# Scales that are powers of two: one chain on VectorE in place of a chain on two engines

## The chip, the cores and the metric

One core of a Trainium2 chip runs the kernel. The metric is device time in microseconds of one execution; runs are compared by their median. The core has a matrix engine (TensorE, "PE" in the profile; its weight loads are "PEld"), VectorE ("DVE"), ScalarE ("ACT"), GpSimd ("POOL") and SyncE ("SP"). Each engine works off its own instructions in the order of the program, and waits on semaphores for the others. In this kernel SP and POOL only issue transfers.

## The reference: a gated long convolution beside a feed-forward layer

For 2048 positions of 1024 channels, with `xn` the layer norm of `A_q`:

```python
k_shift = sum(k_pad[:, t:t + S, :] * shift_k[:, ks - 1 - t] for t in range(ks))   # four taps
kv = k_shift * v
y = irfft(rfft(kv_pad) * rfft(ssm_k_pad))[:S] + kv * ssm_D     # causal convolution over 2048 positions
A = xn * y
B = silu(xn @ w1) @ w2                                         # 1024 -> 3584 -> 1024
return A_q + A + B
```

All is in float32. The kernel gets there with half-precision matmuls: each operand is multiplied by a scale and split into a float16 high part and a float16 remainder, and three products of these parts are summed. The scales are powers of two, so they change nothing but the exponent, and they are found from the data: squares are summed, the sum's exponent is halved by shifting its bits, and the result and its reciprocal become the factors by which parts are scaled and outputs scaled back.

## The kernel before: streams, an order made by a planner, and the scales

**Order.** The program is written as some thirty Python generators ("streams"), each of which yields operations (class `Op`) and conditions (tokens and flags). A planner (class `Order`, lines 118 to 206) keeps a clock for each engine. Again and again it takes the operation that could start first by its estimate, less a bias of its stream (0.0 to 0.26 us), emits it, and moves the engine's clock by the operation's estimated time. That gives one fixed order of instructions for each engine. An estimate that changes can so move instructions that have nothing to do with it. An `Op` may emit several instructions, which then stand together.

**Stages.** First the layer norm, transposes and splits of x. Beside it the 14 column pairs of `w1` are loaded, squared and summed, scaled and split (`scales_w1`, line 713, and `factors_w1`, line 762); pairs 0 and 1 are used as they are, the other twelve in a seven-product form of a 2 x 2 block product. TensorE runs `xn @ w1` in two halves (lines 941 to 1017), then the product with `w2` (lines 1045 to 1064), and at the end eight units of the seven-product form (`units2`, line 1092). ScalarE and VectorE evacuate its results, split them again, and make the parts of `w2`.

**The convolution** runs beside this from some 200 us on, in eight groups of 128 channels (line 1350 and after). For each group: `gate` (line 1407) applies the taps and multiplies by v, with squares summed on ScalarE; `signal_parts` splits; `stage1` makes the first part of a transform on TensorE, and `to_spec` copies it out; `forward`, `product` and `inverse` are long VectorE instructions on the tile `spec`; `energy` sums squares of the product on ScalarE; `result_scales` (line 1617) makes the scales of the result; `result_parts` splits; `stage1_inv` transforms back on TensorE; `gated` (line 1719) applies scales row tile by row tile, multiplies by the normed x, and writes out. From the fifth group on that write is a transfer that adds to the output in DRAM, issued by POOL.

**The end.** The last unit of the feed-forward part (`evacuate2`, lines 1139 to 1184) reads one output tile back (line 1175), after all convolution outputs are there (flag "conv out"), adds it to its own result, and writes without adding. Its other results go out as adding transfers from POOL, in the same queue as those of the convolution.

**The scales.** Two routines make them. `norm` (line 446): a matmul with ones sums over the partitions into PSUM; then one `Op` on VectorE reduces, takes the maximum with 1e-30, shifts, and runs the caller's `then`, all in one piece. `norm_on_two` (line 482): the same matmul; ScalarE sums up the columns (each sum an activation and a read of the accumulator, with the tile `tiny` as a bias that keeps the sum above zero); VectorE shifts and takes a reciprocal (lines 495 and 497); ScalarE multiplies by constants (`small`, line 478, one activation each, L480 in the profile). `norm` serves w1's pairs 0 and 1 and the norm of w2; `norm_on_two` serves the pairs after that (twelve), the gate (eight) and the result (eight). The factors go into `wsc` for w1 and into `csc` (`sc` in the code) for a group; columns 8 to 23 of `sc` hold the result's factor times each row tile's reciprocal deviation (`rstd`), which `gated` takes as scales.

Of the kernel before, what the change touches and what calls it, by code (L numbers as in the profile page):

```python
# [11 lines left out]
F32 = mybir.dt.float32  # L12
BF16 = mybir.dt.bfloat16
F16 = mybir.dt.float16
I32 = mybir.dt.int32
AF = mybir.ActivationFunctionType
ALU = mybir.AluOpType
AX = mybir.AxisListType
ADD, SUB, MUL = ALU.add, ALU.subtract, ALU.mult

P = 128
# [9 lines left out]
W = 512  # L31
# [269 lines left out]
def h3_ffn_kernel(ctx, tc, x, kp, vs, fs, shift, dskip, w1, w2, cfwd, cinv, out):  # L301
# [23 lines left out]
    def V(f, o, ins, us=None, m=0.15):  # L325
        return Op("DVE", us or 1.03 * (size(o) / 960 + 0.075), 0.16, f, ins, [o], m)
# [4 lines left out]
    def T(f, o, ins, us, m=0.1):  # L331
        return Op("PE", us, 0.3, f, ins, [o], m)
# [22 lines left out]
    def a_act(o, i, func, scale=1.0, bias=None, total=None):  # L355
        def f():
            kw = {} if bias is None else {"bias": bias}
            if total is not None:
                kw["accum_out"] = total
            nc.scalar.activation(o, i, func, scale=scale, **kw)  # L360
        ins = [i] + [s for s in (scale, bias) if s is not None and not isinstance(s, float)]
        p = A(f, o, ins)
        p.table = func if func in (AF.Silu, AF.Sqrt) else None
        p.busy += 0.07 * (len(ins) - 1) - 0.06 * (i.space == bass.MemoryType.PSUM)
        if total is not None:
            p.busy += 0.19
            p.writes.append(total)
        return p
# [29 lines left out]
    for n, e in enumerate((14 - 64, 10 - 64, 8 - 64, 64 - 23, 64)):  # L398
        nc.vector.memset(powers[:, n:n + 1], 2.0 ** e)
    invc = cst.tile([P, 1], F32, name="invc")  # L400
    tiny = cst.tile([P, 1], F32, name="tiny")
    nc.vector.memset(tiny, 2.0 ** -100)
    eps = cst.tile([P, 1], F32, name="eps")
    nc.vector.memset(eps, EPS)
    one = cst.tile([P, 1], F32, name="one")
# [40 lines left out]
    def norm(ring, ss, ns, then, flags, margin=1.5):  # L446

        yield ring.ready
        pt, tok = ring.tile([P, W])
        yield pw.ready  # L450
        e, etok = pw.tile([P, 16])

        cols, n = len(ns), sum(ns)

        def mm():
            nc.tensor.matmul(pt[:, 0:n], ones, ss, start=True, stop=True)

        def chain():
            for c, m in enumerate(ns):
                q = sum(ns[:c])  # L460
                if m > 1:
                    nc.vector.tensor_reduce(e[:, c:c + 1], pt[:, q:q + m], axis=AX.X, op=ADD)
                else:
                    nc.vector.tensor_copy(e[:, c:c + 1], pt[:, q:q + 1])
            pow2(e[:, 0:cols], e[:, 0:cols])
            then(e[:, 0:cols])

        yield T(mm, pt[:, 0:n], [ss], 0.25, m=margin)
        p = V(chain, e, [pt[:, 0:n]], us=1.1)
        p.writes = p.writes + flags[0]  # L470
        yield p
        tok.set()
        etok.set()
        for t in flags[1]:
            t.set()


    def small(o, i, scale, ins=()):

        return Op("ACT", 0.2, 0.2, lambda: nc.scalar.activation(o, i, AF.Copy, scale=scale), [i, *ins], [o], 0.15)  # L480

    def norm_on_two(ring, ss, ns, then, flags, margin=1.5):

        yield ring.ready
        pt, tok = ring.tile([P, W])
        yield pw.ready
        e, etok = pw.tile([P, 16])
        cols, n = len(ns), sum(ns)

        def mm():  # L490
            nc.tensor.matmul(pt[:, 0:n], ones, ss, start=True, stop=True)

        def halved():
            a, r = e[:, 0:cols], e[:, 2:2 + cols]
            nc.vector.tensor_scalar(a.bitcast(I32), a.bitcast(I32), 24, 23,
                                    op0=ALU.logical_shift_right, op1=ALU.logical_shift_left)
            nc.vector.reciprocal(r, a)

        yield T(mm, pt[:, 0:n], [ss], 0.25, m=margin)
        for c, m in enumerate(ns):  # L500
            q = sum(ns[:c])
            p = a_act(e[:, 8:8 + m], pt[:, q:q + m], AF.Identity, 1.0, tiny, total=e[:, c:c + 1])
            p.busy = 0.4
            yield p
        tok.set()
        yield V(halved, e[:, 0:4], [e[:, 0:2]], us=0.34)
        yield from then(e[:, 0:cols], e[:, 2:2 + cols])
        etok.set()
        for t in flags:
            t.set()  # L510


# [200 lines left out]
    def scales_w1():  # L713
        for n, (_, i) in enumerate(pairs):
            yield (0.25, 0.16, 0.1, 0.05)[min(n, 3)]
            m = 4 if n < 2 else 2
            if n >= NP:
                for a in range(m):
                    yield flag["raw", n, a]
                flag["scaled", n].set()  # L720
                continue
            yield sq_r.ready
            ss, tok = sq_r.tile([P, 4])
            for a in range(m):
                yield flag["raw", n, a]
                r = raws[n][2][a]
                yield a_act(junk[:, 0:r.shape[1]], r, AF.Square, total=ss[:, a:a + 1])

            def then(e, i=i):
                sc = wsc[:, i]  # L730
                nc.vector.tensor_scalar(sc[:, 3:5], powers[:, 3:5], e, None, op0=MUL)
                nc.vector.reciprocal(e, e)
                nc.vector.tensor_scalar(sc[:, 0:3], powers[:, 0:3], e, None, op0=MUL)
            if n < 2:
                yield from norm(ctxs["nm"], ss[:, 0:m], (m,), then, ([wsc[:, i]], [flag["scaled", n], tok]))
                continue

            def scales(e, r, i=i):
                sc = wsc[:, i]
                yield small(sc[:, 3:5], powers[:, 3:5], e, [e])  # L740
                yield small(sc[:, 0:3], powers[:, 0:3], r, [r])
            yield from norm_on_two(ctxs["nm"], ss[:, 0:m], (m,), scales, [flag["scaled", n], tok])

    spills = []

# [604 lines left out]
    def convolution(floor):  # L1350
# [56 lines left out]
        def gate():  # L1407

            for g in range(NG):
                yield csc_r.ready  # L1410
                scs[g] = sc, _ = csc_r.tile([P, 8 + NT])
                yield css_r.ready
                sss[g] = ss, _ = css_r.tile([P, 12])
                yield flag["kf", g]
                kf, _ = kfs[g]
                yield acc_r.ready
                accs[g] = acc, _ = acc_r.tile([P, 2, T2, P])
                for a in range(2):
                    yield hi_r.ready
                    j, tok = hi_r.tile([P, T2, P], BF16)  # L1420
                    yield a_act(j, kf[:, a], AF.Square, total=ss[:, 4 + a:5 + a])
                    tok.set()

                flag["acc", g].set()
                tap = [taps[:, g, j:j + 1] for j in range(TAPS)]
                for b in range(2):
                    yield flag["kin", g, b]
                    kin, tok = kins.pop((g, b))
                    o = acc[:, b]
                    yield a_act(o, kin[:, 0:T2], AF.Copy, tap[HALO])  # L1430
                    for j in (2, 1, 0):
                        yield v_stt(o, kin[:, HALO - j:HALO - j + T2], tap[j], o, MUL, ADD)
                    tok.set()
                    for q in range(2):
                        yield flag["v", g, b, q]
                        v, tok = vals.pop((g, b, q))
                        o = acc[:, b, q * TQ:(q + 1) * TQ]
                        yield v_tt(o, o, v, MUL)
                        yield a_act(v, o, AF.Square, total=ss[:, 2 * b + q:2 * b + q + 1])
                        tok.set()  # L1440

                def scales(e, r):
                    yield small(sc[:, 0:2], r, 2.0 ** (15 - 64))
                    yield small(sc[:, 2:4], e, 2.0 ** 64)
                    yield small(sc[:, 6:7], sc[:, 2:3], sc[:, 3:4], [sc[:, 3:4]])
                yield from norm_on_two(py_r, ss[:, 0:6], (4, 2), scales, [flag["scales", g]], 4.0)

        CB = 0.03

# [167 lines left out]
        def result_scales(g):  # L1617

            yield flag["energy", g]
            sc, ss = scs[g][0], sss[g][0]  # L1620

            def scales(e, r):
                yield small(sc[:, 4:5], r, 2.0 ** (15 - 64 - 50))
                yield small(sc[:, 7:8], e, -2.0 ** (64 - 41))
                yield small(sc[:, 5:6], sc[:, 7:8], sc[:, 6:7], [sc[:, 6:7]])
                yield small(sc[:, 8:], rstd, sc[:, 5:6], [sc[:, 5:6]])
            yield from norm_on_two(py_r, ss[:, 8:12], (4,), scales, [flag["un", g], sss[g][1]], 3.0)

        def inverse(g):

# [223 lines left out]
```

## Time and profile before

| | |
|---|---|
| Median of 3 runs | 1256.85 us (1254.98 to 1257.09) |
| The profiled execution | 1258.14 us, its span 1256.4 us |
| Granted TensorE clock, mean | 0.994 |
| TensorE, VectorE, ScalarE, GpSimd busy | 1232.6, 1117.9, 790.5, 83.5 us |
| Squares summed, first to last scale of w1 | shifts at 55.7 to 255.4 us |
| Gate and result scales of the groups | shifts at 275.5 to 1197.5 us |

In the profile an instruction is named by its line, engine and operation, and by the tiles that it writes and reads (`out<-in`, without buffer numbers). Lines 336, 346, 349, 352 and 360 are helpers that record most instructions, so there the tile tells which it is. The time is followed by the mean of one in ns and by the idle time of the engine before it, with what ended it: `[1.05 <-ACT py L360]` says that the engine stood idle for 1.05 us and went on when ScalarE's instruction on tile `py` had finished. Matmuls overlap: one is shown with 0.38 us, while the next one starts 0.21 to 0.22 us after it. On VectorE too, an instruction that doesn't need the one before can start ahead of its end.

### The profile page before, as it was taken

How to read it: one execution, taken by the hardware profiler on the slowest of the kernel's cores; microseconds unless marked ns; L12 is line 12 of the kernel's file. 1: busy time of each engine (PE TensorE's matmuls, PEld its weight loads, DVE VectorE, ACT ScalarE, POOL GpSimd, SP SyncE). 2: the span in 40 equal slices, each digit the busy share in tenths (PEclk: the TensorE clock that was granted, in tenths of full speed). 3: DMA queues.
4: the chain of work that ended last, by engine and by line, in shares of the span. 5: the costliest groups of instructions: out<-in, count | busy, mean ns of one | idle time of the engine just before them, and what ended most of it. 6: DMA issues, size and time to landing. Idle time of an engine off the chain costs nothing. (4 is left out here: it accounts for less than half of the span.)

```text
span 1256.4 us, 17146 instructions
## 1 busy us (share of the span) xinstructions
PE 1232.6 (98%) x6034; PEld 597.5 (48%) x6034; DVE 1117.9 (89%) x1359; ACT 790.5 (63%) x1431; POOL 83.5 (7%) x93
## 2 busy tenths in 40 slices
PE   7999999999999999999999999999999999999996
PEld 6554444444444544444444544544544544454452
DVE  7999987997999789998999899799989889988970
ACT  7868888886588878568654643744653545563351
POOL 0000000000000000000000000000120030123132
PEclk8999999999999999999999999999999999999999
DMA  9276989989799899769984655688595497969765
GB/s 367 82 262 239 315 288 303 300 240 227 232 336 270 242 309 313 207 191 297 311 278 125 206 179 132 185 269 231 107 257 153 106 225 217 243 137 161 164 121 80
DMA packets 272662, 279.83 MB, mean 223 GB/s; under 512 B 73792, under 2 KB 192576, under 8 KB 271296
## 3 DMA queue, kind: packets, MB, share of 16 engines
q1 hardware_dynamic: 256848, 262.22, 67.9%
q0 software_dynamic: 15728, 16.52, 9.9%
q8 instruction: 47, 0.77, 0.3%
q14 instruction: 39, 0.32, 0.1%
HBM read 175.66 MB, written 88.34 MB: 210 GB/s over the span
## 5 line engine op out<-in xcount | busy, mean ns | idle before, releaser
L1074 PE MATMUL ff<-x,wo 128*128 128x512 f16 x864 | 327.9, 380 | 3.4 <-ACT hf L360 3.4
L1076 PE MATMUL ff<-x,wo 128*128 128x512 f16 x864 | 328.1, 380 | 0.0
L1075 PE MATMUL ff<-x,wo 128*128 128x512 f16 x864 | 327.9, 380 | 0.1
L946 PE MATMUL ff<-x,wo 128*128 128x512 f16 (+1 forms) x808 | 304.5, 377 | 6.2 <-ACT hf L360 3.0
L948 PE MATMUL ff<-x,wo 128*128 128x512 f16 (+1 forms) x808 | 304.8, 377 | 1.0 <-DVE wo L352 1.0
L947 PE MATMUL ff<-x,wo 128*128 128x512 f16 (+1 forms) x808 | 304.8, 377 | 0.0
L349 DVE TENSOR_TENSOR spec<-spec 128x512 f32<-128x512 f32 (+2 forms) x256 | 261.8, 1053 | 2.0
L1075 PEld LDWEIGHTS <-wo 128*128 128x128 f16 x864 | 84.6, 98 | 104.0 <-issue 4.7
L1076 PEld LDWEIGHTS <-wo 128*128 128x128 f16 x864 | 84.6, 98 | 102.6 <-issue 1.0
L1074 PEld LDWEIGHTS <-wo 128*128 128x128 f16 x864 | 85.5, 99 | 100.1 <-issue 0.6
L948 PEld LDWEIGHTS <-wo 128*128 128x128 f16 x808 | 79.6, 98 | 94.3 <-DVE wo L352 1.5
L947 PEld LDWEIGHTS <-wo 128*128 128x128 f16 x808 | 79.5, 98 | 93.8 <-issue 5.8
L946 PEld LDWEIGHTS <-wo 128*128 128x128 f16 x808 | 81.0, 100 | 90.2 <-ACT wo L360 1.7
L349 DVE TENSOR_TENSOR tmp<-spec 128x2048 f32<-128x2048 f32 (+1 forms) x48 | 92.7, 1933 | 0.9
L352 DVE SCALAR_TENSOR_TENSOR ht<-hf,wsc,ht 128x1024 f16<-128x1024 f32 (+1 forms) x56 | 67.4, 1203 | 7.5 <-ACT ht L360 7.2
L360 ACT ACTIVATE spec<-ps 128x512 f32<-128x512 f32 x92 | 53.2, 592 | 28.7 <-PE ps L1522 28.0
L352 DVE SCALAR_TENSOR_TENSOR wo<-raw,wsc,wo 128x512 f16<-128x512 f32 (+1 forms) x56 | 56.4, 1012 | 11.9 <-ACT wo L360 11.9
L346 POOL DMA_DIRECT2D out<-hf x47 | 45.8, 981 | 303.9 <-ACT hf L360 254.4
L360 ACT ACTIVATE hf<-ff,invc 128x512 f32<-128x512 f32 x32 | 21.9, 684 | 65.7 <-PE ff L1076 47.6
L360 ACT ACTIVATE ht<-hf,wsc 128x1024 f16<-128x1024 f32 (+1 forms) x56 | 60.8, 1085 | 3.4 <-DVE hf L349 2.1
L360 ACT ACTIVATE spec<-spec 128x1024 bf16<-128x1024 f32 x32 | 33.7, 1054 | 46.1 <-DVE spec L349 46.0
L349 DVE TENSOR_TENSOR spec<-tmp 128x512 f32<-128x512 f32 (+1 forms) x80 | 61.3, 792 | 0.7
(188 smaller groups left out, 1779.3 us busy)
## 6 DMA issues: line engine op xcount, KB each, us to landing
wo<-hs SPq DMA_DIRECT2D x160, 256.0 KB, 3.2
hs<-ht SPq DMA_DIRECT2D x80, 256.0 KB, 4.8
raw<-in_w SPq DMA_DIRECT2D x28, 512.0 KB, 5.9
wraw<-in_w SPq DMA_DIRECT2D x24, 512.0 KB, 5.4
w2n<-in_w SPq DMA_DIRECT2D x24, 512.0 KB, 6.1
out<-hf POOLq DMA_DIRECT2D x47, 256.0 KB, 4.5
kin<-in_kp SPq DMA_DIRECT2D x16, 704.0 KB, 5.1
xt<-in_x SPq DMA_DIRECT2D x16, 512.0 KB, 7.3
```

The source lines that it names most:

```text
L346: return Op("POOL", 1.1, 3.0, lambda: nc.gpsimd.dma_start(o, i, accum_op=ADD), [i], [o], m, 2.3 * n)
L349: return V(lambda: nc.vector.tensor_tensor(o, a, b, op=op), o, [a, b], **k)
L352: return V(lambda: nc.vector.scalar_tensor_tensor(o, a, s, b, op0=op0, op1=op1), o, [a, b] + ([] if isinstance(s, float) else [s]), **k)
L360: nc.scalar.activation(o, i, func, scale=scale, **kw)
L946: nc.tensor.matmul(o, w[:, 0, k], xf[:, :, k, 0], start=first and k == 0, stop=False, **kw)
L947: nc.tensor.matmul(o, w[:, 0, k], xf[:, :, k, 1], start=False, stop=False, **kw)
L948: nc.tensor.matmul(o, w[:, 1, k], xf[:, :, k, 0], start=False, stop=last and k == KH - 1, **kw)
L1074: nc.tensor.matmul(po, hx[:, n, 0, :], wc[:, n, 0, :], start=first and n == 0, stop=False, **kw)
L1075: nc.tensor.matmul(po, hx[:, n, 0, :], wc[:, n, 1, :], start=False, stop=False, **kw)
L1076: nc.tensor.matmul(po, hx[:, n, 1, :], wc[:, n, 0, :], start=False, stop=last and n == 3, **kw)
```

## The change

`norm_on_two`, `small` and the constant `tiny` go. Their three callers use `norm`, each with a `then` that holds its scales as VectorE instructions. The result's last instruction makes the factors of all 16 row tiles, as ScalarE's did.

```diff
@@ scales_w1
-            if n < 2:
-                yield from norm(ctxs["nm"], ss[:, 0:m], (m,), then, ([wsc[:, i]], [flag["scaled", n], tok]))
-                continue
-
-            def scales(e, r, i=i):
-                sc = wsc[:, i]
-                yield small(sc[:, 3:5], powers[:, 3:5], e, [e])
-                yield small(sc[:, 0:3], powers[:, 0:3], r, [r])
-            yield from norm_on_two(ctxs["nm"], ss[:, 0:m], (m,), scales, [flag["scaled", n], tok])
+            yield from norm(ctxs["nm"], ss[:, 0:m], (m,), then, ([wsc[:, i]], [flag["scaled", n], tok]))
@@ gate
-                def scales(e, r):
-                    yield small(sc[:, 0:2], r, 2.0 ** (15 - 64))
-                    yield small(sc[:, 2:4], e, 2.0 ** 64)
-                    yield small(sc[:, 6:7], sc[:, 2:3], sc[:, 3:4], [sc[:, 3:4]])
-                yield from norm_on_two(py_r, ss[:, 0:6], (4, 2), scales, [flag["scales", g]], 4.0)
+                def then(e):
+                    nc.vector.reciprocal(sc[:, 0:2], e)
+                    nc.vector.tensor_scalar(sc[:, 0:2], sc[:, 0:2], 2.0 ** (15 - 64), None, op0=MUL)
+                    nc.vector.tensor_scalar(sc[:, 2:4], e, 2.0 ** 64, None, op0=MUL)
+                yield from norm(py_r, ss[:, 0:6], (4, 2), then, ([sc[:, 0:4]], [flag["scales", g]]), 4.0)
@@ result_scales
-            def scales(e, r):
-                yield small(sc[:, 4:5], r, 2.0 ** (15 - 64 - 50))
-                yield small(sc[:, 7:8], e, -2.0 ** (64 - 41))
-                yield small(sc[:, 5:6], sc[:, 7:8], sc[:, 6:7], [sc[:, 6:7]])
-                yield small(sc[:, 8:], rstd, sc[:, 5:6], [sc[:, 5:6]])
-            yield from norm_on_two(py_r, ss[:, 8:12], (4,), scales, [flag["un", g], sss[g][1]], 3.0)
+            def then(e):
+                nc.vector.reciprocal(sc[:, 4:5], e)
+                nc.vector.tensor_scalar(sc[:, 4:5], sc[:, 4:5], 2.0 ** (15 - 64 - 50), None, op0=MUL)
+                nc.vector.scalar_tensor_tensor(sc[:, 5:6], e, -2.0 ** (64 - 41), sc[:, 2:3], op0=MUL, op1=MUL)
+                nc.vector.tensor_tensor(sc[:, 5:6], sc[:, 5:6], sc[:, 3:4], op=MUL)
+                nc.vector.tensor_scalar(sc[:, 8:], rstd, sc[:, 5:6], None, op0=MUL)
+            yield from norm(py_r, ss[:, 8:12], (4,), then, ([sc[:, 4:]], [flag["un", g], sss[g][1]]), 3.0)
```

For the planner each site was a matmul of 0.25 us, one or two ScalarE operations of 0.4 us, one on VectorE of 0.34 and two to four of 0.2 on ScalarE; it becomes the matmul and one VectorE operation of 1.1 us. On the engines a w1 pair has six VectorE instructions in place of two, a gate seven, a result eight, and four, seven and six fewer on ScalarE. The matmul, its PSUM tile and the transfers are the same.

More of the change, by code (lines that the diff above doesn't have):

```diff
@@ L400, in h3_ffn_kernel @@
     invc = cst.tile([P, 1], F32, name="invc")
-    tiny = cst.tile([P, 1], F32, name="tiny")
-    nc.vector.memset(tiny, 2.0 ** -100)
     eps = cst.tile([P, 1], F32, name="eps")
@@ L474, in norm @@
         for t in flags[1]:
[L475 to L509, printed above, removed]
             t.set()
```

## The prediction

> **What bounds the kernel now.** I read the page first, then the engines' busy time by stretch, then what TensorE waited for, and last the end of the timeline.
>
> ```profile
> PE 1232.6 (98%) x6034; PEld 597.5 (48%) x6034; DVE 1117.9 (89%) x1359; ACT 790.5 (63%) x1431; POOL 83.5 (7%) x93
> ```
> ```profile
> 40.00:100.00 60.00, 58.48 (x315) 31.97 (x314) 59.11 (x109) 44.20 (x78) 0.00 (x0) 1.00 0.52 171
> 100.00:300.00 200.00, 200.00 (x950) 93.34 (x948) 177.38 (x235) 166.25 (x263) 0.94 (x1) 1.00 0.89 281
> 300.00:1200.00 900.00, 894.56 (x4324) 423.63 (x4322) 832.07 (x913) 530.94 (x1001) 64.28 (x68) 1.00 0.78 217
> 1200.00:1257.00 57.00, 45.91 (x229) 22.42 (x226) 18.77 (x22) 17.81 (x31) 17.61 (x18) 0.94 0.61 94
> ```
> ```profile
> PE ff L1074 <- ACT hf L360: 3.4, 2, 2.7
> PE ff L946 <- ACT hf L360: 3.0, 1, 3.0
> ...
> PE ff L946 <- DVE hf L349: 1.8, 1, 1.8
> ```
>
> The columns after the length are busy us (and count) of PE, PEld, DVE, ACT and POOL, then the granted clock. TensorE is the bound: between 100 and 1200 us it is busy for all but 5.4 of 1100 us, and outside the start and the end its waits are few. Its work doesn't change here, so before the tail the change can save only those few us. VectorE is the next resource: 98% busy from 40 to 100 us (59.11 of 60), 89% from 100 to 300, 92% from 300 to 1200 (832.07 of 900). ScalarE is at 83% from 100 to 300 and 59% after. The change loads the second fullest engine and unloads one with room. So the question is how late VectorE's long job, the convolution, gets, and whether the kernel's end hangs on it.
>
> The end:
>
> ```profile
> 1221.86 0.69 DVE L349 TENSOR_TENSOR ht<-py,ht 128x512 f32<-128x512 f32 x1 [1.05 <-ACT py L360]
> ...
> 1243.98 0.75 DVE L352 SCALAR_TENSOR_TENSOR hf<-ff,invc,hf 128x512 f32<-128x512 f32 x1 [14.60 <-ACT hf L360]
> 1248.84 0.69 DVE L349 TENSOR_TENSOR hf<-hf 128x512 f32<-128x512 f32 x1 [4.11 <-DMA hf<-out]
> 1249.64 0.75 DVE L352 SCALAR_TENSOR_TENSOR hf<-ff,invc,hf 128x512 f32<-128x512 f32 x1
> ```
> ```profile
> 1230.07 1.11 POOL L346 DMA_DIRECT2D out<-ht  x1 [3.27 <-issue]
> ```
> ```profile
> 1245.45 0.33 SPq L336 DMA_DIRECT2D hf<-out  x1
> ```
> ```profile
> out<-ht POOLq DMA_DIRECT2D x16, 128.0 KB, 4.4
> ```
>
> The convolution's last multiplication (line 1731) ends at 1222.55. Its last accumulating transfer is issued from POOL's queue at 1230.07 and lands some 4.4 us after the issue ends, at about 1230.07 + 1.11 + 4.4 = 1235.6. The last unit of the feed-forward part then reads one output tile back (line 1175, at 1245.45). It may do so only once every convolution output has landed. The tile read back is added at 1248.84, and the last evacuation follows at 1249.64. The read-back was in fact held by the evacuation at 1243.98 and not by the convolution, so the convolution's end has 1245.45 - 1235.6 = **9.8 us of slack**. What it is late beyond that goes into the end one to one.
>
> **The change part by part.** Three callers of the two-engine routine (12 pairs of w1 columns, 8 gates, 8 results) now use the one-chain routine.
>
> ```profile
> 12.24 0.15 DVE L462 TENSOR_REDUCE pow<-nm 128x1 f32<-128x4 f32 x1
> 12.43 0.15 DVE L442 TENSOR_SCALAR pow<-pow 128x1 f32<-128x1 f32 x1
> 12.62 0.15 DVE L443 TENSOR_SCALAR pow<-pow 128x1 int32<-128x1 int32 x1
> 12.80 0.23 DVE L731 TENSOR_SCALAR wsc<-powers,pow 128x2 f32<-128x2 f32 x1
> 13.07 0.16 DVE L732 RECIPROCAL pow<-pow 128x1 f32<-128x1 f32 x1
> 13.27 0.23 DVE L733 TENSOR_SCALAR wsc<-powers,pow 128x3 f32<-128x3 f32 x1
> 13.40 1.28 DVE L352 SCALAR_TENSOR_TENSOR x<-ft,x 128x512 f16<-128x512 f32 x2
> ```
> ```profile
> 55.73 0.14 DVE L495 TENSOR_SCALAR pow<-pow 128x1 int32<-128x1 int32 x1
> 55.91 0.16 DVE L497 RECIPROCAL pow<-pow 128x1 f32<-128x1 f32 x1
> 55.99 1.26 DVE L352 SCALAR_TENSOR_TENSOR ht<-hf,wsc,ht 128x1024 f16<-128x1024 f32 x1
> ```
> ```profile
> 496.80 0.15 DVE L1254 TENSOR_SCALAR invc<-pow 128x1 f32<-128x1 f32 x1
> 496.87 0.15 DVE L1255 RECIPROCAL q<-pow 128x1 f32<-128x1 f32 x1
> ```
>
> The first block is the whole chain that the w1 pairs will run; pairs 0 and 1 run it already. From its first start to the next instruction's it holds VectorE for 13.40 - 12.24 = 1.16 us. The pair of instructions that it replaces holds it for 55.99 - 55.73 = 0.26. That is +0.90 for each of 12 w1 pairs, **10.8 us**.
>
> The other two chains aren't in the trace, so I add steps: 0.19 from an instruction to one that needs its result (12.43 to 12.62) and 0.08 to one that doesn't (496.80 to 496.87 is 0.07, 55.91 to 55.99 is 0.08).
> - Gate, seven instructions: the two reductions 0.08 apart, then 0.19 each to maximum, shift and reciprocal, 0.19 to the first scale, 0.08 to the second, 0.08 to whatever follows: 1.00. Less 0.26 that is +0.74, times 8: **5.9 us**.
> - Result, eight instructions: three steps of 0.19 (to maximum, shift, reciprocal), then 0.19, 0.08, 0.19, 0.19 for the four scales, 0.08 to the next: 1.30. Less 0.26 that is +1.04, times 8: **8.3 us**. Fully dependent (eight steps of 0.27, the largest in the block, 12.80 to 13.07) it would be 2.16, or +15.2 in all; fully independent 0.64, or +3.0.
>
> The sum is 25.0 us of VectorE time. The matmul on TensorE, its PSUM tile and all DMAs stay; a 0.06 us fill of the constant `tiny` at the start goes, ahead of a first matmul batch that waits for loads anyway, so I count nothing.
>
> How much delays the convolution? The 16 gate and result chains (14.2) lie in VectorE's own stretch, ahead of or inside the transforms. I count them whole. The w1 chains lie before 300 us, where VectorE has 0.9 + 22.6 us idle and the feed-forward products are fed through buffers. I take them as covered, and keep 10.8 for the range if that cover fails. ScalarE's relief:
>
> ```profile
> L360 ACT ACTIVATE pow<-py,tiny 128x4 f32<-128x4 f32 x16 | 4.1, 257 | 15.1 <-PE py L491 15.0
> ...
> L480 ACT ACTIVATE csc<-pow 128x1 f32<-128x1 f32 x16 | 2.3, 192 | 12.5 <-DVE pow L497 12.5
> ```
> ```profile
> ACT csc L480 <- DVE pow L497: 20.4, 11, 4.2
> ...
> ACT pow L360 <- PE py L491: 15.2, 11, 3.4
> ```
>
> Each site takes four to seven short instructions off ScalarE, and its 20.4 us of standing behind VectorE's pair goes. What could gain is VectorE waiting for ScalarE:
>
> ```profile
> DVE spec L349 <- ACT spec L360: 31.9, 16, 5.4
> DVE tmp L349 <- ACT spec L360: 13.2, 16, 2.0
> ```
>
> Those 45 us (300 to 1200) come where a group begins and ScalarE copies fresh sums out of PSUM, one after the other with VectorE and TensorE. The removed instructions sit at the gate and at the result, elsewhere in a group, so I take 0 and keep a gain of up to 5 (a tenth of it). The wait for the matmul moves too: ScalarE paid 15.2 us of it, and now VectorE stands there, with the transforms queued behind. But VectorE reached its pair late enough nearly every time:
>
> ```profile
> DVE pow L495 <- ACT pow L360: 0.9, 2, 0.6
> ```
>
> It waited in 2 of 28 cases, and ScalarE's sums came after the matmul. So I take 0; the other end is the whole 15.2.
>
> The convolution is late by 14.2, less 9.8 of slack: **+4.4 us**. On the profiled execution (span 1256.4, its own time 1258.14) that is a span of 1260.8 and a time of 1262.5; the median shown is 1.3 below that execution, so **1261.3** is the forecast.
>
> **Rivals.**
>
> 1. *Covered.* VectorE's 67.9 us idle from 300 to 1200 takes up a third of the 14.2, the delay stays within the 9.8, and TensorE ends as before: 1255 to 1259, about 1257. For it: TensorE's 98%. Against: that idle time is waiting in single steps, and work queued at another place doesn't fall into it.
>
> 2. *Faster.* Every instruction is placed by a planner that gets other costs (1.1 us of VectorE for 0.34, no ScalarE), so the order shifts everywhere. If ScalarE's freed time brings its evacuations ahead of TensorE, the waits of 3.4 and 3.0 us above go, each with a slow stretch after it:
>
> ```profile
> 588.00 0.40 PE L946 MATMUL ff<-x,wo 128*128 128x512 f16 x1 [2.96 <-ACT hf L360]
> 588.22 0.61 PE L947 MATMUL ff<-x,wo 128*128 128x512 f16 x1
> 588.62 0.63 PE L948 MATMUL ff<-x,wo 128*128 128x512 f16 x1
> ...
> 591.61 0.40 PE L1520 MATMUL ps<-hi,cfw 128*128 128x512 f16 x1
> 591.84 0.38 PE L1521 MATMUL ps<-lo,cfw 128*128 128x512 f16 x1
> ```
>
> After 2.96 us of idleness eight matmuls follow in 591.61 - 588.22 = 3.39 us, 0.42 apart, where later ones are 0.22 apart: 1.6 us lost on top. Both waits and two such stretches are 3.4 + 3.0 + 3.2 = 9.6 us; with two thirds of it the time is 1250.5. Against it: no scale instruction stands in front of those evacuations, and the late one, at 1239, comes from the transfer queue:
>
> ```profile
> 1238.29 0.69 ACT L360 ACTIVATE hf<-ff,invc 128x512 f32<-128x512 f32 x1 [10.94 <-DMA out<-hf]
> ```
>
> 3. *TensorE starves in the middle.* VectorE at 92% goes to (832.07 + 14.2)/900 = 94%. Where it falls behind the plan, a feed-forward evacuation comes late and TensorE, in order, stands. Three more waits of 3 us with their slow stretch are 3 x 4.6 = 13.8 us, with the tail 4.4: about 1275. For it: the wait of 1.8 us on VectorE exists already. Against: one such wait in 1100 us. [...] The trace shows the half rate after 2.96 us already, so I keep 1.6 each.
>
> **How the numbers follow.** Forecast 0.45, covered 0.20, faster 0.15, starved 0.20. The forecast's own range: with the result chain's ends (+3.0 to +15.2 for 8.3) and a third of the w1 chains it is -0.9 to +15 us, 1256 to 1272. Nothing covered and all matmul waits paid by VectorE would be 25.0 + 15.2 - 9.8 = +30.4, or 1287; that and gains over 7 us are what I leave out. The range is 1250 to 1278. A measurement of this kernel tells about 0.2% (2.5 us) from no change, so below 1254.3 is faster and above 1259.4 slower: faster 0.15, same 0.22 (covered, and the forecast's low edge), slower 0.63.
>
> **What would show it.** Right: VectorE busy up by about 25 us and ScalarE down by over 30; TensorE's busy time nearly unchanged; the last convolution multiplication some 14 us later; the read-back of line 1175 waiting for the convolution's last transfer; the feed-forward evacuation before it no longer the one that holds it. The w1 step is wrong if TensorE waits for weight factors before 300 us. The zero for the matmul's wait is wrong if the reductions of line 462 have idle time of VectorE before them. The whole is wrong if the time grows while the convolution ends no later, with the loss in TensorE's waits in the middle, or if TensorE's own last product ends earlier than before.

## The result and the profile after

The changed kernel takes 1264.27 us (median of 5 runs, 1262.11 to 1268.25) against 1256.85 (5 runs, 1254.98 to 1258.74): a ratio of 1.0062, 95% interval 1.0038 to 1.0085. It is 7.4 us slower. The forecast was 4.4 us. Its profiled execution took 1264.27 us with a span of 1262.2, which is 5.8 us longer than the span of before.

The page of the changed kernel, its engines; the busy time by stretch; and TensorE's waits (lines after the removed routines have moved up, so L1029 to L1031 are the products called L1074 to L1076 before, and L1475 is the old L1520):

```profile
PE 1232.6 (98%) x6034; PEld 597.3 (47%) x6034; DVE 1137.6 (90%) x1494; ACT 765.1 (61%) x1279; POOL 83.5 (7%) x93
```
```profile
40.00:100.00 60.00, 57.32 (x308) 31.25 (x307) 58.70 (x116) 41.96 (x65) 0.00 (x0) 1.00 0.49 162
100.00:300.00 200.00, 197.00 (x928) 90.99 (x927) 180.70 (x273) 153.24 (x211) 0.94 (x1) 1.00 0.88 273
300.00:1200.00 900.00, 890.59 (x4303) 421.59 (x4301) 829.31 (x976) 515.27 (x907) 63.41 (x67) 1.00 0.78 217
```
```profile
...
PE ff L1030 <- DVE x L352: 2.6, 2, 2.0
PE py L1668 <- DVE zl L352: 1.9, 2, 1.6
...
PE ps L1475 <- ACT tmp L360: 1.6, 3, 1.1
...
PE ff L1029 <- ACT x L360: 1.4, 1, 1.4
```

TensorE has the same 1232.6 us of work. But between 40 and 1200 us it is now busy for 1144.9 us, where it was busy for 1153.0 before: 8.1 us less, of which 7.5 us are now behind 1200 us. They went in many places. One of the largest is this one, where the last units of the feed-forward part begin (first row before, second row after; TensorE's busy time and number of matmuls come first):

```profile
1095.00:1115.00 20.00, 19.86 (x96) 9.23 (x95) 19.86 (x27) 8.99 (x18) 3.85 (x5) 1.00 0.72 154
```
```profile
1095.00:1115.00 20.00, 16.00 (x66) 6.74 (x65) 19.76 (x23) 7.83 (x14) 2.59 (x3) 0.91 0.64 144
```

Thirty matmuls fewer start in these 20 us; at 0.216 us each that is 6.5 us. The waits for `x` listed above (2.6 us for VectorE and 1.4 for ScalarE) all lie around here, and the granted clock of 0.91 takes up to 1.8 us more (0.09 of 20 us). Not all of this lasts to the end: TensorE's last matmul, shown further down, comes 4.8 us later.

The end, after:

```profile
1240.22 0.69 DVE L349 TENSOR_TENSOR ht<-py,ht 128x512 f32<-128x512 f32 x1 [2.19 <-ACT py L360]
1248.80 0.75 DVE L352 SCALAR_TENSOR_TENSOR hf<-ff,invc,hf 128x512 f32<-128x512 f32 x1 [7.89 <-ACT hf L360]
1254.82 0.69 DVE L349 TENSOR_TENSOR hf<-hf 128x512 f32<-128x512 f32 x1 [5.26 <-DMA hf<-out]
1255.61 0.75 DVE L352 SCALAR_TENSOR_TENSOR hf<-ff,invc,hf 128x512 f32<-128x512 f32 x1
```
```profile
1244.58 1.09 POOL L346 DMA_DIRECT2D out<-ht  x1 [1.28 <-issue]
```
```profile
1250.79 0.33 SPq L336 DMA_DIRECT2D hf<-out  x1
```

The convolution's last multiplication ends at 1240.91, which is 18.4 us later than before, and its last transfer (`out<-ht`) is issued at 1244.58, 14.5 us later. The view of transfers gives the time from a transfer's issue to its landing. For this transfer and for the last feed-forward transfer ahead of the read-back (`out<-hf`, issued at 1241.48 before and at 1246.53 after), the first two rows are of before, the other two of after:

```profile
out<-ht POOLq DMA_DIRECT2D x1, 128.0 KB, 3.4
```
```profile
out<-hf POOLq DMA_DIRECT2D x1, 256.0 KB, 3.9
```
```profile
out<-ht POOLq DMA_DIRECT2D x1, 128.0 KB, 3.2
```
```profile
out<-hf POOLq DMA_DIRECT2D x1, 256.0 KB, 4.2
```

So the convolution's last output lands at about 1230.07 + 3.4 = 1233.5 before and 1244.58 + 3.2 = 1247.8 after. The feed-forward transfer lands at about 1241.48 + 3.9 = 1245.4 and 1246.53 + 4.2 = 1250.7, and the read-back goes out right behind it, at 1245.45 and 1250.79. The waits of SyncE's queue from 1225 us on say the same, before and after:

```profile
SPq L336 <- DMA out<-hf: 37.2, 1, 37.2
```
```profile
SPq L336 <- DMA out<-hf: 33.4, 1, 33.4
```

The read-back needs a buffer of the ring `hf`, from which the feed-forward transfers are written. In neither kernel did it wait for the convolution. TensorE's own last matmul, before and after:

```profile
1248.96 0.38 PE L1076 MATMUL ff<-x,wo 128*128 128x512 f16 x1
```
```profile
1253.78 0.38 PE L1031 MATMUL ff<-x,wo 128*128 128x512 f16 x1
```

It starts 4.8 us later. From its start to the last evacuation it was 0.7 us before and is 1.8 now. So of the 5.8 us of span 4.8 are TensorE's delay and only some 1.1 lie behind it, where the last evacuation now waits for the tile read back.

### The profile page after: what moved, and what is told of

It reads as the page before. It is cut to its first block, busy times and chain, and to the rows that moved or that the text cites. A ratio compares the mean times of both kernels' runs of the same rounds, so it can differ in the third digit from the quotient of the medians.

```text
span 1262.2 us, 17124 instructions
## 1 busy us (share of the span) xinstructions
PE 1232.6 (98%) x6034; PEld 597.3 (47%) x6034; DVE 1137.6 (90%) x1494; ACT 765.1 (61%) x1279; POOL 83.5 (7%) x93
## 4 chain that ended last, share of the span: by engine, by line
PE 59%; DVE 24%; issue 8%; DMA 4%; ACT 4%; POOL 1%; SPq 0%; POOLq 0%; ACTq 0%; DVEq 0%
PE ff L903 10%; PE ff L901 10%; PE ff L902 10%; DVE spec L349 8%; PE ff L1030 7%; PE ff L1031 7%; PE ff L1029 7%; DVE tmp L349 3%; DVE x L352 2%; DVE acc L352 2%; PE ps L1475 2%; PE ps L1477 2%; PE ps L1476 2%; DVE spec L352 1%; DMA w2n<-in_w 1%
## 5 line engine op out<-in xcount | busy, mean ns | idle before, releaser
L1030 PE MATMUL ff<-x,wo 128*128 128x512 f16 x864 | 328.2, 380 | 2.6 <-DVE x L352 2.6
L1029 PE MATMUL ff<-x,wo 128*128 128x512 f16 x864 | 328.0, 380 | 2.2 <-ACT x L360 1.4
L1031 PE MATMUL ff<-x,wo 128*128 128x512 f16 x864 | 328.1, 380 | 0.0
L1031 PEld LDWEIGHTS <-wo 128*128 128x128 f16 x864 | 84.6, 98 | 105.2 <-issue 3.7
L1030 PEld LDWEIGHTS <-wo 128*128 128x128 f16 x864 | 84.6, 98 | 102.2 <-issue 3.5
L1029 PEld LDWEIGHTS <-wo 128*128 128x128 f16 x864 | 85.6, 99 | 99.9 <-issue 0.8
L352 DVE SCALAR_TENSOR_TENSOR acc<-kin,taps,acc 128x1024 f32<-128x1024 f32 x48 | 61.3, 1276 | 3.8 <-ACT acc L360 3.8
L360 ACT ACTIVATE wo<-raw,wsc 128x512 f16<-128x512 f32 (+1 forms) x56 | 51.8, 927 | 20.2 <-DVE raw L349 8.3
```

The source lines that it names most:

```text
L352: return V(lambda: nc.vector.scalar_tensor_tensor(o, a, s, b, op0=op0, op1=op1), o, [a, b] + ([] if isinstance(s, float) else [s]), **k)
L1029: nc.tensor.matmul(po, hx[:, n, 0, :], wc[:, n, 0, :], start=first and n == 0, stop=False, **kw)
L1030: nc.tensor.matmul(po, hx[:, n, 0, :], wc[:, n, 1, :], start=False, stop=False, **kw)
L1031: nc.tensor.matmul(po, hx[:, n, 1, :], wc[:, n, 0, :], start=False, stop=last and n == 3, **kw)
```

## The experiments

Three theories were on trial. **Tail**, the prediction's: VectorE's time delays the convolution, and the end hangs on the read-back. **Stall**: VectorE's time makes TensorE wait in the middle, and the end follows TensorE's last product. **Order**: the planner, given other estimates, puts instructions elsewhere, and that alone moves the time. Each run is compared with runs of the kernel before on the same chip.

| Run | Median us | Ratio to before, 95% interval | us |
|---|---|---|---|
| w1 pairs alone on one chain | 1271.69 | 1.0116 (1.0099 to 1.0134) | +14.8 |
| gate and result alone on one chain | 1253.17 | 0.9976 (0.9967 to 0.9985) | -3.7 |
| before, padded at all sites | 1268.17 | 1.0096 (1.0081 to 1.0111) | +11.3 |
| changed, no read-back | 1264.48 | 1.0067 (1.0051 to 1.0082) | +7.6 |
| before, padded at w1 | 1259.15 | 1.0026 (1.0010 to 1.0041) | +2.7 |
| before, padded at gate and result | 1263.29 | 1.0056 (1.0039 to 1.0072) | +6.8 |
| before, planner told more at w1 | 1268.24 | 1.0094 (1.0080 to 1.0108) | +11.7 |
| result alone on one chain | 1260.99 | 1.0032 (1.0019 to 1.0045) | +4.5 |
| before, planner told more at gate and result | 1256.98 | 1.0004 (0.9994 to 1.0015) | +0.2 |
| changed, planner told less at w1 | 1267.48 | 1.0081 (1.0063 to 1.0099) | +10.7 |
| gate and result alone, told 1.0 and 1.3 | 1253.47 | 0.9974 (0.9962 to 0.9985) | -3.3 |
| gate and result alone, told 0.34 | 1260.09 | 1.0033 (1.0018 to 1.0047) | +3.3 |

### The change in two halves

Each half is the change's own edit at the one kind of site, with the other kind left as before.

> The one-chain scales for the twelve w1 pairs alone; gate and result as before. Tail theory (VectorE's added time delays the convolution, and the end hangs on the read-back): the 10.8 us reach the convolution whole, since its first split of results came 12.7 us later in the changed kernel; less 9.8 us of slack, +1 us. Stall theory (VectorE's added time makes TensorE wait in the middle, and the end follows TensorE's last product): a share of 10.8/25.0 of the +7.4, so +3.2 us. Order theory (the planner's new order moves waits about, whatever VectorE's time): no fixed sign, up to 8 us either way.

> The one-chain scales for gate and result alone (16 chains); w1 as before. Tail theory: 14.2 us later, less 9.8: +4.4 us. Stall theory: 14.2/25.0 of +7.4: +4.2 us. With the run of w1 alone the two add up to +7.4 by the stall theory, to +5.4 by the tail theory. Order theory: the two don't add up.

Measured: +14.8 and -3.7. The first is more than any of the three theories allowed. The loss sits wholly with the twelve w1 chains, which the prediction took as covered; the sixteen gate and result chains, which it counted in full, come out faster than before. Tail and stall theories both gave positive sums for the second half, so VectorE's time alone can't be the account. The two halves add up to +11.1 and the whole change is +7.4, so they don't quite add.

The first split of convolution results tells how far the convolution had come. The groups are of the kernel before, of w1 alone, and of gate and result alone; "415.0 to" is the first start:

```profile
L352 DVE SCALAR_TENSOR_TENSOR zl<-spec,csc,zh x32: 1276/1280/1286, 415.0 to 1213.4; 128x1024 f16<-128x1024 f32 x32
```
```profile
L352 DVE SCALAR_TENSOR_TENSOR zl<-spec,csc,zh x31: 1273/1277/1285, 429.7 to 1226.3; 128x1024 f16<-128x1024 f32 x31
```
```profile
L352 DVE SCALAR_TENSOR_TENSOR zl<-spec,csc,zh x32: 1274/1278/1286, 413.8 to 1221.0; 128x1024 f16<-128x1024 f32 x32
```

With w1 alone the convolution is 14.7 us late from its first group on, more than the 10.8 us that were added. With gate and result alone it starts on time.

### VectorE's time alone, in the old order

```diff
         nc.vector.reciprocal(r, a)
+        for k in range(more):      # 5 at a w1 pair, 4 at a gate, 5 at a result
+            nc.vector.tensor_scalar(e[:, 12:13], e[:, 2 if k == 0 else 12:3 if k == 0 else 13], 1.0, None, op0=MUL)
```

> The kernel before, with dependent dummy instructions of one element behind VectorE's pair (5 at a w1 pair, 4 at a gate, 5 at a result: 132, some 25 us), of which the planner isn't told. ScalarE's part and the order of every other instruction stay. Tail and stall theories: the same as the change, +6 to +9 us, the tail theory with TensorE's waits as before and a late read-back, the stall theory with 5 to 9 us more of TensorE's waits before 1200 us. Order theory: 0 to +1 us.

> The kernel before, with 5 dependent dummy instructions behind VectorE's pair at the twelve w1 pairs alone (11.4 us), the planner not told, the order unchanged: VectorE's time alone, without the new order. Cost theory (the +14.8 us of the run with w1 alone is VectorE's time): +10 us or more. Order theory (it is the new place of the instructions): 0 to +4 us, the part of the +11.3 us of the fully padded kernel that 11.4 of 25 us make being at most 5.

> The same with 4 dummies at a gate and 5 at a result alone (13.7 us). Cost theory: what gate and result chains cost in VectorE's time is here without ScalarE's relief: +5 to +9 us, so that the -3.7 us of the run with gate and result alone came from ScalarE's relief or from the order. If VectorE's time at these places is covered: 0 to +2 us.

Measured: +11.3, +2.7 and +6.8. In the traces of all three, TensorE, VectorE and ScalarE take the other instructions in exactly the order of before. So VectorE's time alone does cost, with all sites padded more than the 6 to 9 us expected, and it costs more where the convolution is than before it: 13.7 us at the gates and results cost 6.8, 11.4 us at w1 only 2.7. The time goes in waits of this kind (the fully padded kernel; its L1522 is L1520 before, where the same wait was 0.6 us in all):

```profile
PE ps L1522 <- ACT tmp L360: 5.7, 3, 2.5
```
```profile
900.08 1.15 ACT L360 ACTIVATE zh<-spec,csc 128x1024 f16<-128x1024 f32 x1 [6.22 <-DVE spec L352]
...
902.84 1.07 ACT L360 ACTIVATE tmp<-ps 128x512 f32<-128x512 f32 x2
903.47 0.38 PE L1522 MATMUL ps<-hi,cfw 128*128 128x512 f16 x1 [2.48 <-ACT tmp L360]
```

The same two instructions before:

```profile
892.31 1.15 ACT L360 ACTIVATE zh<-spec,csc 128x1024 f16<-128x1024 f32 x1 [5.28 <-DVE spec L352]
...
895.70 0.38 PE L1520 MATMUL ps<-hi,cfw 128*128 128x512 f16 x1 [0.59 <-ACT tmp L360]
```

ScalarE waited here for VectorE before, too (5.28 us), and now waits longer (6.22 us). The copy out of PSUM that frees a tile `ps` (`tmp<-ps`, 1.07 us for two) stands behind that in ScalarE's order, and TensorE, whose order has a transform matmul next, stands for 2.48 us in place of 0.59. Slack at the end doesn't prevent such a wait.

### The read-back taken out

```diff
-        last = u == len(tiles2) - 1
+        last = False
```

> The changed kernel with its last unit writing all its results as adding transfers: no output is read back, and nothing waits for the convolution's outputs. Tail theory: 4 to 6 us faster than the changed kernel (1258 to 1260). Stall theory: the trace shows the last evacuation 1.2 to 1.5 us behind what TensorE alone allows, so at most 1.5 us faster (1263 to 1264).

Measured: 1264.48 us (6 runs, 1259.04 to 1267.03), the same as the changed kernel's 1264.27, and its trace has the changed kernel's order up to the end. The tail theory falls: with nothing left that waits for the convolution's outputs, the time is the same. The last evacuation of this kernel waits for TensorE (the trace is of the fastest of the six runs):

```profile
1250.13 0.75 DVE L352 SCALAR_TENSOR_TENSOR hf<-ff,invc,hf 128x512 f32<-128x512 f32 x1 [4.65 <-PE ff L1031]
```

### The order alone

```diff
-        yield V(halved, e[:, 0:4], [e[:, 0:2]], us=0.34)
+        yield V(halved, e[:, 0:4], [e[:, 0:2]], us=1.1)       # at the w1 pairs; in the other run at gate and result
```

> The kernel before, in which the planner alone is told that VectorE's pair takes 1.1 us instead of 0.34 at the twelve w1 pairs; no instruction is added or removed. Order theory: a good part of the +14.8 us, +5 to +15 us. Cost theory: within 2 us of the kernel before.

> The kernel before, in which the planner alone is told 1.1 us instead of 0.34 for VectorE's pair at gates and results; no instruction is added or removed. The run with gate and result chains was -3.7 us, VectorE's time there alone +6.8, so something else is worth -10.5. Order theory: it is the new order, so about -10 us here. Relief theory: it is ScalarE's freed time, so within 2 us of the kernel before.

Measured: +11.7 for w1 and +0.2 (no difference) for gate and result, where the order theory had about -10. The first is the clearest run of the study. Not one instruction is added, VectorE is as busy as before, and the kernel is 11.7 us slower. What the order does, by the first split of results and by the stretch that stood out above:

```profile
L352 DVE SCALAR_TENSOR_TENSOR zl<-spec,csc,zh x31: 1272/1279/1285, 431.6 to 1224.8; 128x1024 f16<-128x1024 f32 x31
```
```profile
1095.00:1115.00 20.00, 15.18 (x54) 6.17 (x53) 19.79 (x27) 8.32 (x19) 3.45 (x4) 0.75 0.59 128
```

The convolution starts 16.6 us later. In the stretch where the last feed-forward units begin, 54 matmuls start instead of 96, and 42 x 0.216 = 9.1 us. Up to 5 of these are the clock's (0.75 granted over 20 us); the rest are waits. That is not a price that always reaches the end: the kernel told more at gate and result starts only 83 matmuls in this stretch and is as fast as before. VectorE is full there in all of these kernels (19.6 to 19.9 of 20 us), so what differs is the order in which it does its work. The timeline of this run:

```profile
1105.73 0.59 PE L1075 MATMUL ff<-x,wo 128*128 128x512 f16 x1 [1.06 <-DVE x L352]
...
1106.31 2.29 DVE L349 TENSOR_TENSOR spec<-spec 128x2048 f32<-128x2048 f32 x1
...
1108.52 0.75 DVE L352 SCALAR_TENSOR_TENSOR x<-x,tau,x 128x512 f16<-128x512 f32 x1
...
1109.32 0.59 PE L1075 MATMUL ff<-x,wo 128*128 128x512 f16 x1 [2.15 <-DVE x L352]
```

TensorE waits for a part of `w2` (`x<-x,tau`), and that stands in VectorE's order behind a 2.29 us instruction of the convolution. The changed kernel shows the same waits (`PE ff L1030 <- DVE x`), and with w1 alone they are there too.

### Other estimates for the chains themselves

The first run is the changed kernel with the planner told 0.34 us for the w1 chains. The other two are gate and result alone, told 1.0 and 1.3 us, and 0.34 for both:

```diff
-        p = V(chain, e, [pt[:, 0:n]], us=1.1)
+        p = V(chain, e, [pt[:, 0:n]], us=us)        # us: an argument of the routine
```

> The changed kernel, with the planner told 0.34 us instead of 1.1 for the chains of the twelve w1 pairs; the instructions are those of the change. If the estimate for w1 costs 11.7 us whatever the rest of the order: about 1252.6, 4 us faster than the kernel before. If each order has its own luck: no relation, anywhere from 1250 to 1270.

> Gate and result chains alone, the planner told 1.0 us for a gate and 1.3 for a result, near what they take, in place of 1.1 for both. If the -3.7 us belong to the chains: within 2 us of that (-6 to -2). If to one order among many: beyond that, either way.

> The same with the planner told 0.34 us for both. The same two readings as for the run with 1.0 and 1.3; and if an estimate that is too low lets VectorE fall behind the plan, TensorE waits more behind convolution copies, as in the padded kernel: +5 us or more.

Measured: +10.7, -3.3 and +3.3. The first expectation failed: telling the planner less doesn't bring the w1 chains' loss back, so the estimate's 11.7 us aren't a fixed price of it. The late start isn't the whole account either: this kernel's first split of results is at 417.0, on time but for 2 us, it starts 95 matmuls between 1095 and 1115 us, and TensorE loses the time at other places. The longest of its waits is for an evacuation:

```profile
PE ff L901 <- DVE hf L349: 3.8, 1, 3.8
```
```profile
L352 DVE SCALAR_TENSOR_TENSOR zl<-spec,csc,zh x32: 1276/1280/1286, 417.0 to 1229.5; 128x1024 f16<-128x1024 f32 x32
```

The gate and result chains keep their gain at the truer estimates (-3.3 against -3.7, intervals overlapping) and lose it when the planner doesn't know of them (+3.3, less than the +5 expected for that case). The kernel told 0.34 (first row below) has the waits of the padded one again, four of them, where the kernel told 1.0 and 1.3 (second row) has two. Between 1095 and 1115 us they start 95 and 96 matmuls, so that stretch isn't the difference between them.

```profile
PE ps L1520 <- ACT tmp L360: 7.6, 4, 2.6
```
```profile
PE ps L1520 <- ACT tmp L360: 2.4, 2, 1.7
```

### The result scales alone

> The one-chain scales for the eight results alone. If the gain of gate and result (-3.7 us) is a matter of each chain, a share of 8.3/14.2: about -2 us. If it is a matter of the order that came out, anything from -5 to +5 us.

Measured: +4.5 us, where gates and results together gave -3.7. By the difference the gate chains would be worth -8.2, which no account of eight chains supports. One site alone isn't a term of a sum: each subset gives its own order. In this run TensorE waits 4.2 us for evacuations by ScalarE in the last units (3.4 before), 1.9 us for parts of `w2` and 2.6 us for the copies of the convolution (0.6 before).

## Why the prediction was right in time and wrong in place

- **VectorE's time was worked out well.** The result chain runs from 1214.52 to the next instruction at 1215.87 in the changed kernel:

```profile
1214.52 0.15 DVE L460 TENSOR_REDUCE pow<-py 128x1 f32<-128x4 f32 x1
...
1215.08 0.16 DVE L1578 RECIPROCAL csc<-pow 128x1 f32<-128x1 f32 x1
1215.28 0.15 DVE L1579 TENSOR_SCALAR csc<-csc 128x1 f32<-128x1 f32 x1
1215.35 0.15 DVE L1580 SCALAR_TENSOR_TENSOR csc<-pow,csc 128x1 f32<-128x1 f32 x1
...
1215.87 0.75 DVE L352 SCALAR_TENSOR_TENSOR hf<-ff,invc,hf 128x512 f32<-128x512 f32 x1
```

  That is 1.35 us, forecast 1.30, with a step of 0.20 to a dependent instruction (1215.08 to 1215.28) and 0.07 to an independent one (1215.28 to 1215.35). A gate's took 1.00, as forecast. VectorE's busy time rose by 19.7 us, less than the 25 of the sum, which counts from start to start. ScalarE's fell by 25.4, not by over 30.
- **The zero for the matmul's wait was right.** VectorE waited for it 1.4 us in all.

```profile
DVE pow L460 <- PE nm L454: 1.1, 1, 1.1
DVE pow L460 <- PE py L454: 0.3, 2, 0.2
```

  The fill of `tiny` was rightly put at nothing, though for another reason than the one given: TensorE's first batch waits not for loads but for a later fill (`one`), 1.2 us before and 1.1 after.

- **The step that failed is "the w1 chains lie before 300 us ... I take them as covered".** They are the part that costs: +14.8 us alone. As VectorE's time in the old order they do cost little (2.7), so most of the cover was there. The step's own sign, TensorE waiting for weight factors before 300 us, hardly shows either (one wait of 0.5 us for a part of `w1` that wasn't there before). What the step left out is that the planner re-orders by its estimate, which alone was worth 11.7 us. In the change, with w1 alone and with the estimate alone the convolution starts 13 to 17 us later (427.7, 429.7 and 431.6 against 415.0). That the late start is what costs isn't shown: the changed kernel told less at w1 starts it at 417.0 and loses 10.7 us.
- **The other step that failed is that the convolution's lateness is paid at the end, beyond 9.8 us of slack.** The convolution did end late (18.4 us). But the read-back waits for a feed-forward transfer in both kernels, and in the change the convolution's last output was there 3.0 us before it went out (1247.8 against 1250.8). The slack was mis-sized too. The prediction added the median of 4.4 us to the end of the issue, where the page counts from the issue, and this transfer took 3.4: the slack before was 1245.45 - 1233.5 = 12.0 us. And what held the read-back then was the transfer that landed at 1245.4, not the evacuation at 1243.98. So its sign that the read-back waits for the convolution's last transfer wasn't met. Without the read-back the time is the same: by then TensorE had lost its time already, its last product coming 4.8 us later. The 4.4 us of the forecast stood at the wrong place, and the agreement with 7.4 owes to chance.
- **The rival "TensorE starves in the middle" named the mechanism**, waits of TensorE in the middle with a slow stretch behind them, but not the place: it had late feed-forward evacuations, and most of the waits that grew in the change are for parts of `w2` and for the convolution's splits and copies. Its price of 13.8 us was near that of the padded kernel (+11.3), and about twice that of the change; the 4.4 us that it added for the tail weren't there.
- **The rival "faster" holds for the gate and result chains.** The two waits that it named, 3.4 and 3.0 us, are 1.4 and 2.2 us there (0.8 and 0.5 with the estimates 1.0 and 1.3). That the gain is ScalarE's relief isn't shown: with the planner told more at gate and result both are 1.7 us, and nothing is gained. Against it as a pure matter of order stands the planner told more with no change of time (+0.2); for a part of relief speaks that chains unknown to the planner cost 3.3 us and dummies unknown to it 6.8, though in different orders. How the 3.5 us divide stays open. So does why the w1 chains keep their loss under either estimate.

The best kernels of the study have the chains at gate and result alone: 1253.17 us, 0.24% faster than before and 0.9% faster than the change, and 1253.47 with the other estimates, no different.

## What to carry to other kernels

Where a planner fixes the order of all engines, a new estimate is an edit of its own. Test it by itself (the same instructions, another number) and test the added work by itself (dummies that the planner doesn't know). Here the first was worth up to 11.7 us with nothing added, about as much as 25 us of VectorE's time. And slack at the end is no cover for an engine that works in order: in the padded kernel TensorE paid for VectorE's lateness where its order had a matmul that depended on it (2.48 us at one such matmul, 0.59 before). Counting the matmuls started per stretch finds such places; whether the loss lasts to the end, TensorE's last matmul tells. Before a slack is counted, look up what let the later instruction go.

## What the runs showed of the hardware that had not been expected

In one run the slow clock came behind three short waits, where before it had come behind one of 2.96 us (at 588.00). It is the run with the planner told more at w1: TensorE had waited 0.34, 1.27 and 1.06 us between 1101.88 and 1105.73 when its matmuls began to follow one another 0.42 us apart instead of 0.22:

```profile
1103.86 0.38 PE L1075 MATMUL ff<-x,wo 128*128 128x512 f16 x1 [1.27 <-DVE x L352]
...
1105.73 0.59 PE L1075 MATMUL ff<-x,wo 128*128 128x512 f16 x1 [1.06 <-DVE x L352]
1106.11 0.64 PE L1076 MATMUL ff<-x,wo 128*128 128x512 f16 x1
1106.53 0.63 PE L1074 MATMUL ff<-x,wo 128*128 128x512 f16 x1
```

The granted clock of the stretch (third number from the end) is 0.50 over 10.2 us:

```profile
1104.80:1115.00 10.20, 7.12 (x18) 2.75 (x18) 9.99 (x14) 3.60 (x10) 1.72 (x2) 0.50 0.49 75
```

And the same long wait was seen without it. Before, the matmul at 588.00 waited 2.96 us, the next one took 0.61 us, and seven more went at half rate. In the kernel padded at w1 the same matmul waits just as long, and the next one takes 0.38 us; the mean granted clock of that execution is 0.997, where before it was 0.994:

```profile
590.73 0.38 PE L948 MATMUL ff<-x,wo 128*128 128x512 f16 x1 [2.96 <-ACT hf L360]
590.94 0.38 PE L949 MATMUL ff<-x,wo 128*128 128x512 f16 x1
```

So the prediction's price of 1.6 us for a slow stretch behind each 3 us wait isn't a fixed one: none is seen behind this wait of the padded kernel, and behind the three short waits it was up to 5 us, an estimate from 10.2 us at a clock of 0.50. What decides between the two isn't shown.
